# New ranks for the tasks of a kernel's opening, and products of a tile of ones on TensorE

## The chip, the cores and the metric

The kernel runs on one core of a Trainium2 chip. The time is that of the device, in microseconds (us), from the start of one execution to its end. Engines are named as the profile names them: PE is TensorE's matmul, PEld its load of the stationary operand, DVE is VectorE, ACT is ScalarE, POOL is GpSimd, and SP is SyncE, whose queue issues the DMAs. L12 is line 12 of the kernel; the changed kernel has a few lines more, so the same code stands some 3 to 15 lines further down there.

## The reference

Eight batches of an attention with two kinds of masks (a window of 32 keys in heads 0 to 3, every fourth of 128 keys in heads 4 to 7) feed a layer that turns the result by learned angles, mixes tokens and then channels:

```python
scores = scale * np.matmul(q, k.transpose(0, 1, 3, 2))
scores = np.where(masks[None, :, :, :], scores, -1000000000.0)
scores = scores - np.max(scores, axis=-1, keepdims=True)
attn = np.exp(scores)
attn = attn / (np.sum(attn, axis=-1, keepdims=True) + 1e-09)
x = np.matmul(attn, v)            # then (B, 8, 576, 64) -> (B, 576, 512)
theta = x @ w_theta
cos_t, sin_t = (np.cos(theta), np.sin(theta))
zr = x * cos_t
zi = x * sin_t
y = np.einsum('ts,bsd->btd', w_tok_r, zr) + np.einsum('ts,bsd->btd', w_tok_i, zi)
u = x + y
return u + np.maximum(u @ w_ch, 0.0)
```

Sequence 576, 512 channels. The four weights arrive as float64 and are turned into float32 on the chip.

## The kernel before, in words

**Work of a batch b.** The heads go in four pairs p. `scores(b, p)` multiplies a pair's queries and keys (PE, tile `s`, two halves of 5 and 4 blocks of 64 columns, the mask added either by products with `mskb` and `idb` on PE or on DVE), takes the row maxima (DVE, `mx`), the exponentials (ACT, `P`), the sums and their reciprocals (DVE, `sm`), and normalizes (POOL, L510). `turn(b, p)` transposes `P` into `pt` by DVE's 32x32 transposes, in batch 0 `flip` does it on PE; two `pt` tiles alternate between the pairs. `pv(b, p)` multiplies with the values (PE, tile `o`), ACT copies it out into `x`. `theta` multiplies `x` with the angle weights (tile `th`, five stripes of tokens in the order 4, 0, 1, 2, 3), `trig` takes sines and cosines on ACT (`g`, `K`) and multiplies by `x` on DVE, and `zsplit` splits each of the nine tiles `z` into a high part `zh` (ACT or DVE) and a low one `zl` (POOL). A unit `token(b, d, g)` is 27 products into a tile `y`, three for each `z` tile, in the order 0, 4, 1, 5, 2, 6, 3, 7, 8; there are eight units, four d in two halves g of the tokens. `residual` adds them to `x` (DVE, L825) and splits the sum into `u` (ACT, POOL). `chan(b, e, g)` is a unit of 12 products into a tile `c`. In names like `s1_3` or `y0_2` the first number is the batch, the second the pair or the d.

**Weights.** Each weight tile is loaded into a stage (`st_wth`, `st_wtk`, `st_wch`), clipped by DVE (L332), changed by ACT (L334 and L340, or DVE L337 for the second), put together by DVE (L342), and split by ACT (L350) and POOL (L352). The token weights are two sets of five tiles; those of the second half g = 1 (`st_wtk1`, split into `late_wt_a` and `late_wt_b`) and the channel weights (`st_wch`, `late_wc`) are staged in tiles that other weights or the first attention have used before: `st_wch0` needs the stage of `st_wtk1_2`, `st_wch1` that of `st_wtk1_3`, `st_wch2` that of `st_wch0`, `st_wch3` that of `st_wch1`. The DMA goes out only when POOL's split of the tile before has ended.

**Order.** What is done ahead of batch 1's own units is the opening: all of batch 0, the weights, the attention and the angles of batch 1, and two pairs of scores of batch 2. Its tasks are generators that name, step by step, an engine and a planned duration. While the program is written, `Order.run` plays them against each other: of the tasks ready for an engine it takes the one with the lowest rank, and pins the instruction at that place of the engine's order. `RANK` holds one number for each kind of task. So ranks change no instruction, only the order in which each engine and SP's queue run them; each engine works strictly in that order and waits where an operand isn't there. From the first product of `scores(2, 2)` on (PE, L468) the order comes from `phase`, written out by hand, and no rank has a say.

Of the kernel before, what the change touches and what calls it, by code (L numbers as in the profile page):

```python
# [8 lines left out]
F32 = mybir.dt.float32  # L9
F32R = mybir.dt.float32r  # L10
BF16 = mybir.dt.bfloat16
# [7 lines left out]
DM = H * D  # L19
# [10 lines left out]
EARLY = ("u0", "u1", "u2", "u3", "xh0")  # L30
LATE = ("u3", "xh1", "xh2", "xh3", "xh0")
LATE2 = ("xh2", "xh3", "xh2", "xh3")
RANK = dict(load=6.64, scores0=1.09, flip=0.01, pv0=1.13, pair=.21, theta_unpack=1.54, theta0=5.3, trig0=2.41,
            token_early=2.55, theta_split=6.42, token_late=6.75, chan=2.1, units=2.95, evacuate=4.49,
            scores1=4.02, scores2=7.3, pv1=8.0, theta1=5.96, trig1=7.42)
STS = (4, 0, 1, 2, 3)


FG0 = {4: ("zl2", "zl6"), 0: ("zl3", "zl7"), 1: ("zh3", "zh7")}
COS_PSUM, SIN_PSUM = True, True  # L40
KORD = (0, 4, 1, 5, 2, 6, 3, 7, 8)
TP0 = {4: "s", 0: "s", 1: "x", 2: "t", 3: "s"}
TP = {4: "t", 0: "s", 1: "s", 2: "t", 3: "s"}

# [17 lines left out]
class Order:  # L62
# [17 lines left out]
    def signal(self, event):  # L80
        self.events[event] = self.now

    def go(self, gen, rank=None):
        if not self.live:
            for _ in gen:
                pass
            return
        self.serial += 1
        t = [self.rank if rank is None else rank, self.serial, self.now, gen, None, 0.0]
        self.tasks.append(t)  # L90
        self.advance(t)
# [60 lines left out]
def build(ctx, tc, qT, kT, vw, wth, wtk, wch, maskb, ident, identb, outT):  # L152
    nc = tc.nc
    cp = ctx.enter_context(tc.tile_pool(name="const", bufs=1))
# [7 lines left out]
    ps_v = ctx.enter_context(tc.tile_pool(name="ps_v", bufs=1, space=PSUM))  # L162
# [7 lines left out]
    def pe(ins):  # L170
        tc.keep_in_program_order(ins)
# [13 lines left out]
    def reserve(tag):  # L185
        taken[tag] = taken.get(tag, -1) + 1
        return taken[tag]

    def take(tag, bufs, n=None):
        n = reserve(tag) if n is None else n  # L190
        if od.live:
            if n >= bufs:
                yield None, ("free", tag, n - bufs)
            if n:
                yield None, ("got", tag, n - 1)
            signal(("got", tag, n))
        return n

    def give(tag, n):
        if od.live:  # L200
            signal(("free", tag, n))

    def bank(tag, name):
        if tag == "v":
            n = yield from take(tag, 1)
            return ps_v.tile([128, 2 * DM], F32, tag=tag, name=name), (tag, n)
        pl, bufs = banks[tag]
        n = yield from take(tag, bufs)
        return pl.tile([128, DM], F32, tag=tag, name=name), (tag, n)
# [205 lines left out]
    def on_pe(b, pr):  # L415
        return b == 0 or (b, pr) in ((1, 2), (1, 3), (2, 0), (2, 1))
# [24 lines left out]
    def scores(b, pr):  # L441
# [161 lines left out]
    def pv(b, pr):  # L603
# [50 lines left out]
    def theta0(st):  # L654
        cs = slice(128 * st, min(128 * st + 128, S))
        n = cs.stop - cs.start
        for c in range(NC):
            yield None, ("wth32", c)
            yield None, ("xe", 0, c)
            if c == 0:  # L660
                if TP0[st] == "s":
                    yield None, ("sc", 0, NP - 1)
                elif TP0[st] in "tm":
                    yield None, ("fl", 0, NP - 1)
                ths[0, st] = yield from bank(TP0[st], f"th0_{st}")
# [170 lines left out]
    def token(b, d, g):  # L836
        yield None, ("z", b, KORD[0])
        yield None, ("wtk", g, KORD[0] // 2)
        ps, rel = yield from bank(unit_bank(b, NC * g + d), f"y{b}_{d}_{g}")
        ps = ps[:, :HS]  # L840
        cs = slice(128 * d, 128 * d + 128)
        n = 0
        for kt in KORD:
            yield None, ("z", b, kt)
            yield None, ("wtk", g, kt // 2)
            zh, zl = zs[b, kt]
            wh, wl = (w[:, HS * (kt % 2):HS * (kt % 2) + HS] for w in wtks[g, kt // 2])
            yield "PE", 369
            for l, r in ((zh, wh), (zh, wl), (zl, wh)):
                pe(nc.tensor.matmul(ps, l[:, cs], r, start=(n == 0), stop=(n == 3 * NK - 1)))  # L850
                n += 1
        signal(("tk", b, d, g))
        go(residual(b, d, g, ps, rel), RANK["evacuate"])

# [14 lines left out]
    def chan(b, e, g):  # L869
# [7 lines left out]
        for c in range(NC):  # L877
# [3 lines left out]
            for l, r in ((wchs[c][0], uh[b, c]), (wchs[c][0], ul[b, c]), (wchs[c][1], uh[b, c])):  # L881
                pe(nc.tensor.matmul(ps, l[:, cs], r[:, ts], start=(n == 0), stop=(n == 3 * NC - 1)))  # L882
                n += 1
        go(finish(b, e, g, ps, rel), RANK["evacuate"])

# [67 lines left out]
    EA, LA, LA2 = ([(t, reserve(t)) for t in ts] for ts in (EARLY, LATE, LATE2))  # L953
    XH = {p: reserve(f"xh{p}") for p in range(NP)}
    UH = {d: reserve(f"u{d}") for d in range(NC)}
    od.live = True
    go(first_loads(), 0)
    go(consts(), 0)
# [100 lines left out]
```

## Time and profile before

| what | value |
|---|---|
| time, median of 3 runs | 578.16 us (577.14 to 578.73) |
| time of the profiled execution | 577.82 us |
| its span, first to last instruction | 576.0 us |
| mean granted TensorE clock | 0.988 |
| busy shares PE, PEld, DVE, ACT, POOL | 96%, 87%, 66%, 60%, 39% |
| DMA | 81.91 MB, mean 142 GB/s |
| start of batch 2's third pair of scores on PE (end of the opening) | 143.01 us |

A row of the profile's timeline has start, duration, engine, line, operation, what it writes and reads, and how many equal ones it stands for; in brackets is the idle time of the engine just before it and what ended that. A row of windows has, for a stretch of time, its length, each engine's busy time and number of instructions, the clock that TensorE was granted (1.00 is full speed), the share of time the DMA engines moved data, and GB/s. A duration on PE overlaps with the next product's; how fast products follow each other is read from their starts.

### The profile page before, as it was taken

The numbers are of one execution on the slowest core, as the hardware profiler recorded it, in microseconds if no ns is written. First come the engines' busy times: TensorE is split into PE (matmuls) and PEld (weight loads), VectorE is DVE, ScalarE is ACT, GpSimd is POOL, SyncE is SP. The second block draws the span as 40 slices with busy tenths as digits, with TensorE's granted clock in tenths as the row PEclk, the third lists the DMA queues.
The fourth block names the chain that finished last, engine by engine and source line by source line (L and its number), as shares of the span: only waits on it lengthen the run. The fifth ranks groups of instructions, "written<-read, shape, count | busy, mean of one in ns | idle before, by whom it ended". The sixth has DMA issues, their size and how long they took to land.

```text
span 576.0 us, 13996 instructions
## 1 busy us (share of the span) xinstructions
PE 550.5 (96%) x5464; PEld 501.6 (87%) x5464; DVE 378.0 (66%) x1156; ACT 345.2 (60%) x939; POOL 222.2 (39%) x206
## 2 busy tenths in 40 slices
PE   5997799999999999999999999999999999999997
PEld 4744688879999899988999899988999899989997
DVE  3879798865666668756776768756775767445112
ACT  1498967768555784369555785359556695266110
POOL 2228855525224352226324253226323353325220
PEclk9999699899999999999999999999999999999999
DMA  8991437601747046540746146550747123321002
GB/s 303 400 368 28 165 105 245 216 0 63 231 150 193 32 162 210 169 127 20 268 143 172 64 148 202 181 136 11 252 146 190 69 83 102 77 89 65 18 1 83
DMA packets 45586, 81.91 MB, mean 142 GB/s; under 512 B 3920, under 2 KB 19024, under 8 KB 45520
## 3 DMA queue, kind: packets, MB, share of 16 engines
q1 hardware_dynamic: 45520, 81.02, 43.7%
q8 instruction: 43, 0.70, 0.5%
q14 instruction: 23, 0.19, 0.1%
HBM read 64.49 MB, written 16.52 MB: 141 GB/s over the span
## 4 chain that ended last, share of the span: by engine, by line
DVE 34%; ACT 30%; PE 25%; issue 5%; POOL 2%; DMA 2%; SPq 0%; ACTq 0%; POOLq 0%; DVEq 0%
DVE pt L525 16%; PE y L850 11%; ACT P L504 11%; PE c L882 6%; PE th L685 3%; DVE P L409 3%; ACT K L698 3%; ACT K L787 3%; DVE xh L599 3%; ACT th L796 2%; ACT zh L644 2%; DVE xq L729 2%; DVE K L789 2%; ACT cos L705 2%; ACT x L581 2%
## 5 line engine op out<-in xcount | busy, mean ns | idle before, releaser
L830 POOL TENSOR_TENSOR u<-x,u 128x288 fp32r<-128x288 f32 x64 | 54.7, 858 | 184.6 <-ACT u L828 184.6
L525 DVE STREAM_TRANSPOSE pt<-P 32x288 f32<-32x288 f32 x224 | 105.1, 469 | 12.0 <-POOL P L510 8.9
L882 PE MATMUL c<-u,late_wc 128*128 128x288 f32 x768 | 110.2, 296 | 2.8 <-DVE x L859 2.8
L882 PEld LDWEIGHTS c<-u,late_wc 128*128 128x128 f32 x768 | 106.0, 188 | 6.8 <-DVE x L859 4.0
L850 PE MATMUL y<-wtkh,zh 128*128 128x288 f32 x288 | 90.3, 314 | 1.1 <-ACT zh L644 1.1
L850 PE MATMUL y<-wtkh,zl 128*128 128x288 f32 x288 | 86.2, 299 | 4.0 <-POOL zl L646 4.0
L646 POOL TENSOR_TENSOR zl<-g,zh 128x512 fp32r<-128x512 f32 x40 | 52.3, 1316 | 97.5 <-ACT zh L644 84.5
L504 ACT ACTIVATE P<-P,mx 128x64 f32<-128x64 f32 x216 | 72.0, 335 | 25.8 <-DVE mx L498 25.8
L850 PE MATMUL y<-wtkl,zh 128*128 128x288 f32 x288 | 85.9, 298 | 0.0
L828 ACT CAST u<-x 128x288 fp32r<-128x288 f32 x64 | 26.9, 429 | 86.2 <-DVE x L825 85.5
L685 PE MATMUL th<-wthh,xh 128*128 128x512 f32 x224 | 74.8, 395 | 0.3 <-DVE g L784 0.3
L850 PE MATMUL y<-late_wt_b,zh 128*128 128x288 f32 x320 | 68.1, 297 | 0.0
L825 DVE TENSOR_TENSOR x<-y,x 128x288 f32<-128x288 f32 x64 | 28.1, 448 | 53.6 <-PE y L850 53.5
L850 PEld LDWEIGHTS y<-wtkh,zl 128*128 128x128 f32 x288 | 55.1, 191 | 4.7 <-POOL zl L646 4.7
L850 PEld LDWEIGHTS y<-wtkh,zh 128*128 128x128 f32 x288 | 54.9, 191 | 4.7 <-ACT zh L644 2.3
L850 PE MATMUL y<-late_wt_a,zh 128*128 128x288 f32 x256 | 56.3, 301 | 0.0
L850 PEld LDWEIGHTS y<-wtkl,zh 128*128 128x128 f32 x288 | 55.1, 191 | 0.3 <-issue 0.3
L510 POOL TENSOR_TENSOR P<-P,sm 128x576 f32<-128x576 f32 x32 | 37.5, 1172 | 41.1 <-DVE sm L508 18.1
L850 PEld LDWEIGHTS y<-late_wt_b,zh 128*128 128x128 f32 x320 | 51.4, 189 | 0.3
L685 PEld LDWEIGHTS th<-wthh,xh 128*128 128x128 f32 x224 | 42.0, 188 | 9.2 <-DVE g L784 0.6
L850 PE MATMUL y<-late_wt_b,zl 128*128 128x288 f32 x160 | 47.4, 296 | 0.0
L581 ACT COPY x<-o 128x576 f32<-128x576 f32 x32 | 29.4, 919 | 28.4 <-PE o L617 19.1
(108 smaller groups left out, 1106.3 us busy)
## 6 DMA issues: line engine op xcount, KB each, us to landing
q<-in_qT_dram SPq DMA_DIRECT2D x32, 576.0 KB, 5.2
va<-in_vw_dram SPq DMA_DIRECT2D x30, 320.0 KB, 3.2
k<-in_kT_dram SPq DMA_DIRECT2D x28, 304.0 KB, 5.5
out_dram<-x SPq DMA_DIRECT2D x28, 288.0 KB, 2.4
vb<-in_vw_dram SPq DMA_DIRECT2D x29, 256.0 KB, 3.8
xd<-xq SPq DMA_DIRECT2D x24, 288.0 KB, 5.1
xn<-xd SPq DMA_DIRECT2D x24, 256.0 KB, 3.4
st_wtk<-in_wtk_dram SPq DMA_DIRECT2D x8, 576.0 KB, 8.8
```

What stands on the lines that cost most here:

```text
L409: pin(nc.vector.tensor_tensor_reduce(out=P[:, n], in0=ps[:, n - g0], in1=mskb[:, mask_of(pr, n)], op0=ALU.add, op1=ALU.max, scale=1.0, sca ...
L504: table(nc.scalar.activation(P[:, n], P[:, n], AF.Exp, bias=mx[:, n:n + 1], scale=SCALE, accum_out=sm[:, n:n + 1]))
L510: pin(nc.gpsimd.tensor_tensor(P, P, sm.unsqueeze(2).to_broadcast([128, NJ, BW]), op=ALU.mult))
L525: pin(nc.vector.transpose(pmats[b, pr][k0:k0 + QB, :, hh, QB * e:QB * e + QB], P[p0:p0 + QB, :, QB * o:QB * o + QB]))
L581: pin(nc.scalar.copy(dst, src))
L646: pin(nc.gpsimd.tensor_tensor(lo, z, hi.bitcast(F32), op=ALU.subtract))
L685: pe(nc.tensor.matmul(pt, l, r, start=(n == 0), stop=(n == 3 * NC - 1)))
L825: pin(nc.vector.tensor_tensor(x[:, ts], ps, x[:, ts], op=ALU.add))
L828: pin(nc.scalar.copy(uh[b, d][:, ts], x[:, ts]))
L830: pin(nc.gpsimd.tensor_tensor(ul[b, d][:, ts], x[:, ts], uh[b, d][:, ts].bitcast(F32), op=ALU.subtract))
L850: pe(nc.tensor.matmul(ps, l[:, cs], r, start=(n == 0), stop=(n == 3 * NK - 1)))
L882: pe(nc.tensor.matmul(ps, l[:, cs], r[:, ts], start=(n == 0), stop=(n == 3 * NC - 1)))
```

## The change

The table `RANK` has new numbers. A tile `ones` (128x512, bf16) is set by DVE at the very start, and 14 products of it with itself go to PE ahead of everything else, into a tile `busy` that uses the PSUM banks of `o`. In the first token unit, `token(0, 0, 0)`, eight more such products stand ahead of the first product with `zh3`, and four ahead of the one with `zl3`. Nothing reads what they write.

```diff
-RANK = dict(load=6.64, scores0=1.09, flip=0.01, pv0=1.13, pair=.21, theta_unpack=1.54, theta0=5.3, trig0=2.41,
-            token_early=2.55, theta_split=6.42, token_late=6.75, chan=2.1, units=2.95, evacuate=4.49,
...
+RANK = dict(load=5.45, scores0=5.38, flip=0, pv0=0.8, pair=0.31, theta_unpack=2.69, theta0=2.39, trig0=2.41,
+            token_early=4.11, theta_split=8.74, token_late=5.88, chan=1.75, units=4.8, evacuate=2.41,
...
+WARM_UP = 14
...
+KEEP_BUSY = {(0, 0, 0, 3, 0): 8, (0, 0, 0, 3, 2): 4}
...
+            if (b, d, g, kt) == (0, 0, 0, KORD[6]):
+                busy = yield from bank("v", "busy")
             yield "PE", 369
-            for l, r in ((zh, wh), (zh, wl), (zl, wh)):
+            for i, (l, r) in enumerate(((zh, wh), (zh, wl), (zl, wh))):
+                for _ in range(KEEP_BUSY.get((b, d, g, kt, i), 0)):
+                    pe(nc.tensor.matmul(busy[0][:, :DM], ones[:, :128], ones, start=True, stop=True))
                 pe(nc.tensor.matmul(ps, l[:, cs], r, start=(n == 0), stop=(n == 3 * NK - 1)))
                 n += 1
+        if b == d == g == 0:
+            give(*busy[1])
...
+    ones = cp.tile([128, DM], BF16, name="ones")
+    nc.vector.memset(ones, 1.0)
+    busy = ps_v.tile([128, 2 * DM], F32, tag="v", name="busy")
+    for n in range(WARM_UP):
+        pe(nc.tensor.matmul(busy[:, :DM], ones[:, :128], ones, start=True, stop=True))
```

The orders show what the ranks move. From `scores(2, 2)` on, PE has the same order before and after. Three places ahead of it follow.

**ACT, from the angles of stripe 2 to the last high part `zh0_3`.** Before:

```order
L350 CAST wthh1_653<-st_wth1_97 128x512
L644 CAST zh0_1_665<-K0_1_597 128x512
L796 ACTIVATE g0_2_642<-K0_2_641 128x512
L350 CAST wthh2_672<-st_wth2_98 128x512
L698 ACTIVATE K0_2_641<-K0_2_641 128x512
L787 ACTIVATE K0_3_686<-th0_3_534 128x512
L705 ACTIVATE K0_2_641<-K0_2_641,halfpi_95 128x512
L350 CAST wthh3_684<-st_wth3_99 128x512
L796 ACTIVATE g0_3_687<-K0_3_686 128x512
L644 CAST zh0_2_713<-K0_2_641 128x512
```

After, up to `zh0_3`:

```order
L708 ACTIVATE K0_2_639<-K0_2_639,halfpi_95 128x512
L701 ACTIVATE K0_3_664<-K0_3_664 128x512
L337 ACTIVATE st_wtk1_0_629<-st_wtk1_0_629 128x576
L708 ACTIVATE K0_3_664<-K0_3_664,halfpi_95 128x512
L647 CAST zh0_2_759<-K0_2_639 128x512
L507 ACT_TABLE_LOAD
L507 ACTIVATE P1_0_559,sm1_0_561<-P1_0_559,mx1_0_560 128x64 x3
L343 ACTIVATE st_wtk1_0_629<-st_wtk1_0_629 128x576
L647 CAST zh0_3_797<-K0_3_664 128x512
```

The splits of three angle weights (`wthh1` to `wthh3`) have moved from among the sines to behind the second half's token weights, some twenty rows further on; `zh0_2` has moved behind the last sine (L705, now L708), and two more steps on `st_wtk1` stand ahead of that sine than before (`st_wtk1_1`'s second and `st_wtk1_0`'s first).

**PE, in the units `y0_2` and `y0_3` of the first half.** The first product with batch 1's values, `o1_0`, stood here before:

```order
L850 MATMUL y0_3_0_956<-wtkh0_515,zl0_0_613 128x288
L617 MATMUL o1_0_904<-pt0_107,va1_0_434 64x64 x10
L617 MATMUL o1_0_904<-pt0_107,vb1_0_435 64x64 x8
L850 MATMUL y0_3_0_956<-wtkh2_569,zh0_4_576 128x288
L850 MATMUL y0_3_0_956<-wtkl2_570,zh0_4_576 128x288
```

After, it stands after nine products of the unit before, ahead of the scores `s1_2`:

```order
L857 MATMUL y0_2_0_913<-wtkh0_532,zl0_1_687 128x288
L620 MATMUL o1_0_919<-pt0_124,va1_0_451 64x64 x10
L620 MATMUL o1_0_919<-pt0_124,vb1_0_452 64x64 x8
L857 MATMUL y0_2_0_913<-wtkh2_571,zh0_5_668 128x288
L857 MATMUL y0_2_0_913<-wtkl2_572,zh0_5_668 128x288
L857 MATMUL y0_2_0_913<-wtkh2_571,zl0_5_669 128x288
L427 LDWEIGHTS idb_94
L427 MATMUL s1_2_0_923<-mskb_93,idb_94 128x64
```

`o1_0` has moved up by 21 products of token units, and `o1_1` in the same way from the 24th to the sixth product of `y0_3`. The scores `s1_2` stand six products earlier, the first half of `s1_3` where it stood, its second half 18 products later, behind the ninth product of the second half's first unit.

**DVE, from the maxima of batch 1's third pair to the first channel weight.** Before:

```order
L525 STREAM_TRANSPOSE pt1_109<-P1_1_724 32x9x32 x2
L430 TENSOR_REDUCE mx1_2_906<-s1_2_0_908 128x5
L525 STREAM_TRANSPOSE pt1_109<-P1_1_724 32x9x32 x2
L438 TENSOR_SCALAR mx1_2_906<-mx1_2_906 128x5
L430 TENSOR_REDUCE mx1_2_906<-s1_2_5_940 128x4
L825 TENSOR_TENSOR x0_2_407<-y0_2_0_883,x0_2_407 128x288
L438 TENSOR_SCALAR mx1_2_906<-mx1_2_906 128x4
L342 SCALAR_TENSOR_TENSOR st_wtk1_2_409<-st_wtk1_2_409 128x576
L342 SCALAR_TENSOR_TENSOR st_wtk1_3_479<-st_wtk1_3_479 128x576
L342 SCALAR_TENSOR_TENSOR st_wtk1_4_698<-st_wtk1_4_698 128x288
```

After:

```order
L345 SCALAR_TENSOR_TENSOR st_wtk1_3_496<-st_wtk1_3_496 128x576
L528 STREAM_TRANSPOSE pt1_126<-P1_1_719 32x9x32 x2
L345 SCALAR_TENSOR_TENSOR st_wtk1_4_672<-st_wtk1_4_672 128x288
L528 STREAM_TRANSPOSE pt1_126<-P1_1_719 32x9x32 x2
L433 TENSOR_REDUCE mx1_2_921<-s1_2_0_923 128x5
L528 STREAM_TRANSPOSE pt1_126<-P1_1_719 32x9x32 x2
L441 TENSOR_SCALAR mx1_2_921<-mx1_2_921 128x5
L433 TENSOR_REDUCE mx1_2_921<-s1_2_5_993 128x4
L335 TENSOR_SCALAR st_wch0_963<-st_wch0_963 128x512
L828 TENSOR_TENSOR x0_2_424<-y0_2_0_913,x0_2_424 128x288
L441 TENSOR_SCALAR mx1_2_921<-mx1_2_921 128x4
```

The joins of `st_wtk1_2` to `st_wtk1_4` (L342, now L345) have moved from behind both maxima to ahead of the first (that of `st_wtk1_2` stands further up, ahead of the last two transposes of `pt0`). The clip of the first channel weight, `st_wch0` (L332, now L335), stood 15 rows behind the second maximum; now it is the next row, and two rows behind it stands the L441 for the second half of `s1_2`, without which ACT can't take those exponentials. The other three channel weights have moved up likewise, and in SP's queue `st_wch0` from behind the second load of batch 2's queries to ahead of the first.

More of the change, by code (lines that the diff above doesn't have):

```diff
@@ L32 @@
 LATE2 = ("xh2", "xh3", "xh2", "xh3")
-RANK = dict(load=6.64, scores0=1.09, flip=0.01, pv0=1.13, pair=.21, theta_unpack=1.54, theta0=5.3, trig0=2.41,
-            token_early=2.55, theta_split=6.42, token_late=6.75, chan=2.1, units=2.95, evacuate=4.49,
-            scores1=4.02, scores2=7.3, pv1=8.0, theta1=5.96, trig1=7.42)
+RANK = dict(load=5.45, scores0=5.38, flip=0, pv0=0.8, pair=0.31, theta_unpack=2.69, theta0=2.39, trig0=2.41,
+            token_early=4.11, theta_split=8.74, token_late=5.88, chan=1.75, units=4.8, evacuate=2.41,
+            scores1=5.5, scores2=2.39, pv1=0.3, theta1=4.18, trig1=3.32)
 STS = (4, 0, 1, 2, 3)
```

## The prediction

> **What bounds the kernel now.** I read the page first, then windows, then PE's waits.
>
> ```profile
> span 576.0 us, 13996 instructions
> PE   5997799999999999999999999999999999999997
> DVE  3879798865666668756776768756775767445112
> PEclk9999699899999999999999999999999999999999
> ```
>
> ```profile
> 62.00:90.00 28.00, 24.74 (x276) 22.31 (x275) 23.80 (x62) 23.19 (x94) 19.35 (x16) 0.90 0.38 127
> 90.00:125.00 35.00, 31.81 (x311) 28.27 (x309) 29.43 (x68) 24.00 (x66) 15.38 (x14) 0.95 0.47 160
> 125.00:150.00 25.00, 24.89 (x240) 22.91 (x242) 13.09 (x41) 20.04 (x46) 12.39 (x11) 1.00 0.26 86
> 150.00:300.00 150.00, 148.91 (x1575) 140.22 (x1570) 107.57 (x383) 89.59 (x265) 52.80 (x50) 1.00 0.50 152
> ```
>
> From slice 10 on PE is full: 148.91 of 150 us, at full clock. That part keeps its order, so nothing can be won there; what counts is when it begins:
>
> ```profile
> 143.01 1.27 PE L468 MATMUL s<-k,q 128*64 128x64 f32 x36
> ```
>
> Ahead of it PE has gaps, and from 62 to 125 us DVE is busy 53.2 of 63 us (23.80 + 29.43), nearly as long as PE. PE's waits from 50 to 143 us, with the number and the longest, and the clock around them:
>
> ```profile
> PE y L850 <- POOL zl L646: 4.0, 3, 1.5
> PE s L424 <- ACT P L485: 3.0, 2, 2.0
> PE y L850 <- ACT zh L644: 1.1, 1, 1.1
> PE xn L759 <- DVE K L750: 1.0, 1, 1.0
> PE th L685 <- DVE g L784: 0.3, 1, 0.3
> ```
>
> ```profile
> 66.70:67.80 1.10, 1.01 (x7) 1.00 0.00 0
> 67.80:71.30 3.50, 3.50 (x17) 0.51 0.00 0
> 71.30:75.30 4.00, 4.00 (x32) 1.00 0.00 0
> 101.50:105.20 3.70, 3.69 (x32) 0.56 0.85 267
> ```
>
> Once the last low part, `zl0_3`, is there (PE goes on at 66.79), PE still loses 3.0 + 1.0 + 0.3 = 4.3 us by waits, 3.5 x 0.49 = 1.7 by half clock behind the waits for the last sines, and 3.7 x 0.44 = 1.6 by half clock behind the wait for scores at 101.51: 7.6 us in all. That is the most that a better order behind `zl0_3` could win.
>
> **The change, step by step.** I follow one quantity: how much later the changed kernel reaches a place with the same work of PE done. Each product of a token unit counts 0.133 us (32 in 4.00 us above), `o` 1.2, a half of scores with masks 0.9 or 0.75.
>
> *The first 14 products.* They run while PE would wait for the first keys.
>
> ```profile
> 7.03 1.34 PE L468 MATMUL s<-first_k,q 128*64 128x64 f32 x20 [3.62 <-DMA first_k<-in_kT_dram]
> 13.63 1.34 PE L468 MATMUL s<-first_k,q 128*64 128x64 f32 x20
> 18.02 0.80 PE L468 MATMUL s<-first_k,q 128*64 128x64 f32 x20
> 10.27 1.35 PE s L468 x20
> ```
>
> No row shows a product of ones. At half clock 288 columns take 3.5/17 = 0.21 to 0.24 us, so 512 take some 0.4 and 14 end by about 7.1 us, at full clock they end at half of that; neither delays the keys of 7.03 by more than the two mask products (0.45). Scores at full clock save 0.54 us for 20. But the second pair's start at 10.27 is set by a DMA (the chain of waits has `first_k` up to there), and the gaps between the loads then open wider, in which the clock may fall again. Bounds: +0.3 (the masks come late) to -1.2 (two of four pairs gain); I take **-0.3**, near the row at 10.27, which the clock can't move.
>
> *ACT up to the last high part.*
>
> ```profile
> 54.85 0.66 ACT L350 CAST wthh<-st_wth 128x512 fp32r<-128x512 f32 x1
> 58.39 0.63 ACT L796 ACTIVATE g<-K 128x512 f32<-128x512 f32 x1 [0.68 <-DVE K L789]
> 60.04 0.72 ACT L334 ACTIVATE st_wtk<-st_wtk 128x576 f32<-128x576 f32 x1
> 60.66 0.71 ACT L705 ACTIVATE K<-K,halfpi 128x512 f32<-128x512 f32 x1
> 62.03 1.28 ACT L504 ACT_TABLE_LOAD   x1
> 64.47 0.62 ACT L644 CAST zh<-K 128x512 fp32r<-128x512 f32 x1
> 65.17 1.57 POOL L646 TENSOR_TENSOR zl<-K,zh 128x512 fp32r<-128x512 f32 x1 [0.61 <-ACT zh L644]
> 66.79 0.40 PE L850 MATMUL y<-wtkh,zl 128*128 128x288 f32 x1 [1.11 <-POOL zl L646]
> ```
>
> Ahead of the last sine (60.66) four casts go (three `wthh`, `zh0_2`), 0.53 to 0.57 each by starts, 2.2 us; two steps of `st_wtk1` come, 0.62 each (60.04 to 60.66): -1.0. Between that sine and `zh0_3` stood 3.8 us; now the sine 0.62, `zh0_2` 0.53, a table load 1.28, three exponentials 1.15 (63.32 to 64.47), L343 0.62: 4.2, so +0.4. The wait of 0.68 at 58.39 is for a DVE step that now has fewer rows ahead of it: -0.5. POOL's `zl0_3` started right behind `zh0_3`, so taking a split off POOL gives nothing more. Sum **-1.1**; with the first term `zl0_3` comes 1.4 earlier.
>
> *Products of ones among the last sines.* Eight and four at 0.2 to 0.4 us stand in two waits of 1.1 us. If they overrun, `y0_0` ends up to 1.5 us later, and if they hold the clock, the 1.7 us at half clock go. I cost both at **nothing**: the cover is the chain on DVE, which starts its transposes 3.1 us behind `zl0_3` (66.79 to 69.88), once ACT, DVE and POOL have finished `P1_0`, and PE gets to wait for them, next paragraph. Without that cover it would be -1.7 to +1.5.
>
> *`o1_0`, and DVE up to the third pair's maxima.*
>
> ```profile
> 68.69 1.15 POOL L510 TENSOR_TENSOR P<-P,sm 128x576 f32<-128x576 f32 x1 [0.61 <-DVE sm L508]
> 69.88 0.95 DVE L525 STREAM_TRANSPOSE pt<-P 32x288 f32<-32x288 f32 x2 [1.02 <-POOL P L510]
> 72.40 1.25 DVE L342 SCALAR_TENSOR_TENSOR st_wtk<-st_wtk 128x576 uint32<-128x576 uint32 x1
> 79.02 0.49 DVE L430 TENSOR_REDUCE mx<-s 128x5 f32<-128x320 f32 x1
> 81.39 1.79 DVE L342 SCALAR_TENSOR_TENSOR st_wtk<-st_wtk 128x576 uint32<-128x576 uint32 x3
> 82.47 0.31 PE L424 MATMUL s<-mskb,idb 128*128 128x64 bf16 x5 [1.04 <-ACT P L485]
> ```
>
> PE gets to `o1_0` 7 + 27 + 9 products behind `zl0_3`, 5.7 us; its `pt0` needs DVE's 3.1, eight transposes at 0.48, `sm` 0.5 and one join of 0.6 to 1.25: 8.3. So PE now waits 2.6 us there, where it waited for nothing before. This costs the end nothing yet, because the maxima `mx1_2` are later still: three joins (1.79 together, longer where POOL works beside them, as at 72.40) have come ahead of them, one transpose pair and one join of 72.40's kind have left: **+1.1**. So the maximum comes at 79.02 - 1.4 + 1.1 = 78.7 and the masks of `s1_3` at 82.2, with `o1_1` (1.2 us) already done: 1.5 us ahead.
>
> *Channel weights among the scores.*
>
> ```profile
> 95.71 0.80 PE L617 MATMUL o<-pt,va 128*64 128x64 f32 x20
> 105.36 0.43 DVE L332 TENSOR_SCALAR st_wch<-st_wch 128x512 f32<-128x512 f32 x1 [1.03 <-DMA st_wch<-in_wch_dram]
> 107.86 0.80 PE L617 MATMUL o<-pt,va 128*64 128x64 f32 x20
> DMA to landing us min/median/max: 3.6/4.7/5.6
> ```
>
> Behind the exponentials of `s1_2`'s first half (end at 82.0) ACT now has two `xh`, one `x`, one split and three steps on `st_wch` (some 0.6 each, like the rows of 54.85 and 60.04) and `u` (0.3), 4.6 us, before those of the second half (1.15): 87.8. PE gets to the second half of `s1_3`, whose bank they free, at 82.2 + 4.5 = 86.7 and waits 1.1: **1.1 us ahead** (I count `s1_3`'s missing half against it). Then POOL normalizes `P1_2` up to 89.4 (1.15 as at 68.69, and 0.45 for `sm`), and DVE's eight transposes (3.85), one maximum (0.4), the clip of `st_wch2` (0.4), one residual and a small row (0.6) take 5.3, with 0.5 for the load: 95.2, where PE waits for `o1_2` since 93.4. The old kernel was there at 95.71, but with `s2_0` done and six products fewer: **0.4 behind**. Next, `o1_3`: from 95.2 DVE has two joins (1.3) and a clip (0.4) of channel weights, `sm` (0.4), what is left of POOL's `P1_3` (0.8), two maxima (0.9), the split of `xh1_2` (0.9), a residual (0.5), eight transposes (3.8) and some 0.5 of handing over, 9.5 us: 104.7; PE waits 1.5. The old kernel was there at 107.86, because it lost 2.0 by the wait at 101.51 and 1.6 by the clock behind it, and had then 9 products fewer but `s2_1` done: **2.8 ahead**.
>
> *To the end of the opening.* Batch 1's angles now come earlier among the channel units, so the waits of 1.0 and 0.3 should go: **3.7 ahead** with what little else differs left out. Of the four new waits (2.6, 1.1, 1.9, 1.5) only the last has PE alone behind it; if the clock falls there as at 101.5, that costs 1.6. I add half: **-2.9**.
>
> The Trainium skill says otherwise of this last term. In "TensorE: Matmul & The Clock Gate", Part 1, the clock goes back to half only after a whole idle window of about 3.4 us; no wait here is that long, so by that rule the sum would be -3.7. In this trace it fell behind waits of 1.1 twice and of 1.95 once, so the measurement decides.
>
> **The sum** stands against the profiled execution, 577.82 us (1.82 around its span): 574.9. The median of the runs shown is 0.34 above it: **575.3**.
>
> **The rivals.** *The new waits are shorter than I made them*: ACT takes casts in gaps, and only the wait at `o1_0` stays. Then -1.4 - 7.6 + 2.6 = -6.4: 571.8. For it speaks that each of my waits adds up rows without seeing where they overlap; against it, DVE's 84% from 62 to 125 us. *All is taken back*: the first products gain nothing (+0.3), DVE's wait at 58.39 stays (+0.5), the last clock fall costs fully (+0.8), the wait for `xn` stays (+1.0): 577.9. For it speaks that each of these is in the old trace. That the change doesn't do what it says, a clock that stays half in spite of the ones, is in it, since I gave little for the clock. *Slower*: DVE, in order, stops at each clip of a channel weight until its load lands. `st_wch0` can be issued only when POOL has split `st_wtk1_2`, at some 77.6 us, and lands 3.6 to 5.6 later, while DVE is there at about 81; I counted 0.5 for each of four. If SP's queue, in which these loads stand behind loads of keys and values, issues them 1.5 us later than POOL allows, DVE loses 4 x 1.5 = 6.0: 581.3. It decides from about 1.2 us on, where 4.6 us are lost and the whole is above 579.9.
>
> **How the numbers follow.** A measurement of this kernel can tell about 0.3% (1.7 us) from no change: faster is below 576.4, slower above 579.9. The forecast has 0.50, its own range 573.4 to 577.2, with 0.08 of that above 576.4. Shorter waits have 0.20, all taken back 0.20, slower 0.10. So faster 0.42 + 0.20 = 0.62, within 0.3% 0.28, slower 0.10. The range takes in the first three cases with their unknowns (1.5 us either way on the outer ones): 570.3 to 579.6.
>
> **What would show it.** PE's timeline: `s2_2`'s start at about 140 us instead of 143.01; scores of 20 products at 0.80 instead of 1.34 from 7 us on, if the ones hold the clock; 1.00 in the window behind `zl0_3`; a wait of some 2.6 us ahead of the first `o` behind it, ended by DVE `pt`; 1 to 2 us ahead of the next scores and values; DVE waiting for `st_wch` by DMA for less than 1 us each. I am wrong if PE has no wait at `o1_0`, if those DMA waits pass 1.2 us each, or if PE's share from 150 us on differs.

## The result, and the profile after

| | before | after |
|---|---|---|
| median of 6 runs each | 577.56 us (576.37 to 578.73) | 581.79 us (580.65 to 582.36) |
| profiled execution, its span | 577.82 us, 576.0 us | 581.52 us, 579.7 us |

The ratio is 1.0071, with a 95% interval of 1.0055 to 1.0088: the changed kernel is slower by 4.2 us, where 2.9 us less was predicted.

From the page of the changed kernel:

```profile
span 579.7 us, 14051 instructions
PE   7897978999999999999999999999999999999997
PEclk9999879999999999999999999999999999999999
```

Its windows, with the columns as before:

```profile
62.00:90.00 28.00, 23.67 (x241) 19.97 (x242) 22.91 (x53) 22.46 (x73) 18.69 (x16) 0.88 0.36 125
90.00:125.00 35.00, 32.13 (x338) 28.93 (x337) 28.96 (x67) 25.57 (x88) 16.77 (x16) 1.00 0.49 157
125.00:150.00 25.00, 23.90 (x180) 21.70 (x179) 15.07 (x43) 17.03 (x32) 11.50 (x9) 1.00 0.18 59
150.00:300.00 150.00, 148.88 (x1595) 140.21 (x1594) 105.17 (x365) 92.60 (x279) 53.78 (x51) 1.00 0.51 156
```

From 150 us on nothing has changed (PE 148.88 of 150 us, before 148.91). The difference lies ahead of it, in the opening, whose end is the start of batch 2's third pair of scores in PE's timeline:

```profile
146.35 1.27 PE L471 MATMUL s<-k,q 128*64 128x64 f32 x36
```

That is 3.34 us later than the 143.01 of before; the span has grown by 3.7. From 62 to 90 us PE gets 241 products done, 35 fewer than before and eleven of them products of ones (a few records of a trace can be missing), at a clock of 0.88; from 90 to 125 it has full clock and makes up a part. PE's waits from 50 to 147 us:

```profile
PE o L620 <- DVE pt L528: 6.1, 3, 3.3
PE s L471 <- DVE K L792: 2.0, 1, 2.0
PE y L857 <- POOL zl L649: 1.3, 2, 1.0
PE xn L762 <- DVE g L753: 1.0, 1, 1.0
PE o L620 <- issue: 0.7, 1, 0.7
```

The waits for `zl`, `zh` and `P` (8.1 us) have shrunk to 1.3. Instead there are now waits of 6.1 for the transposes, ahead of the products with the values, 0.7 at the same place whose end the profile doesn't explain ("issue" stands for that), and 2.0 for the angles' `K`.

### The profile page after: what moved, and what is told of

It reads as the page before. It is cut to its first block, busy times and chain, and to the rows that moved or that the text cites. A ratio compares the mean times of both kernels' runs of the same rounds, so it can differ in the third digit from the quotient of the medians.

```text
span 579.7 us, 14051 instructions
## 1 busy us (share of the span) xinstructions
PE 554.4 (96%) x5489; PEld 502.3 (87%) x5490; DVE 380.1 (66%) x1157; ACT 345.7 (60%) x939; POOL 221.4 (38%) x206
## 4 chain that ended last, share of the span: by engine, by line
DVE 34%; ACT 28%; PE 28%; issue 5%; POOL 2%; DMA 2%; SPq 0%; POOLq 0%; ACTq 0%; DVEq 0%
DVE pt L528 16%; PE y L857 11%; ACT P L507 10%; PE c L891 6%; DVE P L412 3%; PE th L688 3%; DVE xh L602 3%; ACT K L701 3%; ACT K L790 2%; ACT th L799 2%; PE th L670 2%; POOL P L513 2%; ACT zh L647 2%; DVE K L792 2%; DVE xq L732 2%
## 6 DMA issues: line engine op xcount, KB each, us to landing
q<-in_qT_dram SPq DMA_DIRECT2D x32, 576.0 KB, 5.0
st_wtk<-in_wtk_dram SPq DMA_DIRECT2D x8, 576.0 KB, 8.5
```

## The experiments

Two causes offered themselves: the new wait at `o1_0` with the half clock behind it (PE; A in the expectations), and the joins that now stand ahead of the third pair's maxima (DVE; B). Later a third came in, ACT's order between the two halves of `s1_2`'s exponentials (E). All ratios are to the kernel before, with 95% intervals; the edits are to the changed kernel unless another is named.

### What of PE, DVE and the products costs it

**e1_hold**: PE is kept busy with 18 products of ones in the wait ahead of `o1_0`, nothing else moves.

```diff
+        if (b, pr) == (1, 0):
+            for _ in range(18):
+                pe(nc.tensor.matmul(ps[:, :DM], ones[:, :128], ones, start=True, stop=True))
         for j in range(NJ):
```

> The changed kernel with 18 more products of ones on PE directly ahead of o1_0, nothing else moved. They fill the wait at o1_0 (73.2 to 76.8 us), so the clock should stay at 1.00 behind it, where it was 0.5 for 5.5 us. Theory A (the loss is PE's wait at o1_0 of 4.0 us and the half clock behind it, 2.8 us): about 2.5 us faster than the changed kernel, 579. Theory B (the loss is DVE's chain, which reaches the first maximum of s1_2 only at 82.2 us, whatever PE does before): 0 to 0.5 us faster, 581.3 to 581.8.

Measured: 581.22 us, 1.0062 (1.0044 to 1.0080). The clock held: from 75.75 to 82.50 us the windows of the changed kernel and of this one read

```profile
75.75:82.50 6.75, 5.69 (x66) 5.04 (x66) 6.21 (x13) 4.40 (x8) 6.75 (x6) 0.50 0.46 159
```

```profile
75.75:82.50 6.75, 6.63 (x102) 5.40 (x101) 6.51 (x12) 4.26 (x8) 6.75 (x6) 1.00 0.51 147
```

so PE had 3.4 us more of full clock, and then stood still. Its timeline, at the masks of `s1_3` and at `o1_2`:

```profile
86.36 0.31 PE L427 MATMUL s<-mskb,idb 128*128 128x64 bf16 x5 [0.71 <-ACT P L488]
...
100.28 1.22 PE L623 MATMUL o<-pt,va 128*64 128x64 f32 x17 [2.31 <-DVE pt L528]
```

The masks come 1.4 us earlier than the 87.79 of the changed kernel, and now with a wait for ACT; `o1_2` comes 0.9 earlier. What PE loses at `o1_0` is at most a small part of what the end waits for: the time is near theory B's, and A's 579 is outside the interval.

**e2_no_joins**: the three joins of `st_wtk1_2` to `st_wtk1_4` are left out.

```diff
-        pin(nc.vector.scalar_tensor_tensor(out=Ti, in0=Ci, scalar=3, in1=Ti,
+        if not (name == "wtk1_" and n >= 2):
+            pin(nc.vector.scalar_tensor_tensor(out=Ti, in0=Ci, scalar=3, in1=Ti,
```

> The changed kernel without the three DVE joins of st_wtk1_2, st_wtk1_3 and st_wtk1_4 (L345; 1.62, 0.86 and 1.21 us in its trace); these weights are therefore not the reference's. All other instructions stand in the same order. Theory A: only the join inside the transposes of pt0 counts, the wait at o1_0 gets 1.6 us shorter and the time falls by 1.6 us, to about 580. Theory B: the first maximum of s1_2 comes 3.7 us earlier, if PE's scores are there, which now come 1.6 us earlier, so 3 us or less are won: 578.5 to 579.5, and the masks of the first half of s1_3 stand near 85 instead of 87.79 us.

Measured: 579.55 us, 1.0040 (1.0026 to 1.0055), about half of the loss given back. In DVE's timeline the first maximum of `s1_2`, and in PE's the two halves of `s1_3`:

```profile
79.02 0.49 DVE L434 TENSOR_REDUCE mx<-s 128x5 f32<-128x320 f32 x1
```

```profile
84.95 0.32 PE L428 MATMUL s<-mskb,idb 128*128 128x64 bf16 x5
...
91.87 0.28 PE L428 MATMUL s<-mskb,idb 128*128 128x64 bf16 x4 [2.01 <-ACT P L489]
```

The maximum is back at the 79.02 of the old kernel, 3.5 us ahead of the changed one, and the first half of `s1_3` 2.8 ahead. But the second half still waits for ACT and comes at 91.87 (92.60 in the changed kernel): a second chain holds there.

**e3_late_o**: `pv1=8.0`, the old rank, in place of the new one, so that the products with batch 1's values stand further back on PE.

> The changed kernel with the rank pv1 as before the change (8.0 instead of 0.3): o1_0 goes behind the scores s1_2 on PE, o1_1 likewise later; DVE keeps its order up to the second maximum of s1_2. Theory A: the wait at o1_0 and the half clock behind it go, 3 to 4 us won, 577.5 to 578.5. Theory B: DVE is at the first maximum at 82.2 us as in the changed kernel, PE only waits later, at the first half of s1_3, for its exponentials until about 86.2 us: 0.3 to 1.6 us won there, 580 to 581.5.

Measured: 582.63 us, 1.0088 (1.0072 to 1.0105). The wait at `o1_0` fell to 0.24 us, and a longer one came at the next place:

```profile
86.62 0.42 PE L427 MATMUL s<-mskb,idb 128*128 128x64 bf16 x5 [5.03 <-ACT P L488]
```

In the changed kernel, in e1 and here, with PE early or late, at full clock or half, these masks come at 87.8, 86.4 and 86.6. So up to here DVE and ACT set most of the time and PE at most the 1.4 us between them, as in e1. The whole came out slower than either theory allowed; what its order costs behind this place was not looked into.

**e4_ranks_only**: the new ranks with no product (the tile and its memset stay).

```diff
-WARM_UP = 14
+WARM_UP = 0
-KEEP_BUSY = {(0, 0, 0, 3, 0): 8, (0, 0, 0, 3, 2): 4}
+KEEP_BUSY = {}
```

> The changed kernel without any product of ones (neither the first 14 nor the twelve among the last sines); the order of everything else is the same. Theories A and B: the half clock behind the last sines comes back (1.7 us), but PE then only waits less at o1_0, and the first scores fall back to 1.34 us for 20, which a DMA hides: 0 to 0.5 us slower than the changed kernel, 581.8 to 582.3. Theory C (the products themselves cost the time): faster by 2 us or more, below 579.8.

Measured: 581.12 us, 1.0056 (1.0043 to 1.0070). Without the products 3.5 of the 4.2 us of loss are still there, so at most a small part of it is theirs.

**e5_ones_only**: the old table `RANK` with all 26 products.

> The kernel before, with its own ranks, plus the products of ones (14 at the start, eight and four among the last sines); the order of everything else is that of before. Theory P (the products win what they fill): the half clock behind the last sines goes (1.7 us) and the time falls to 576. Theory D (DVE's chain to the maxima of s1_2 hides PE's clock there): within 0.5 us of before, 577.1 to 578.1. Theory C (the products cost time): above 578.5.

Measured: 579.66 us, 1.0030 (1.0014 to 1.0046). They didn't help the old order either: slower by 1.6 us, though its profiled execution had full clock throughout the opening.

### ACT's order, and the channel weights

Why the second half of `s1_3` is late shows in ACT's timeline of the changed kernel, where the exponentials of `s1_2`'s two halves begin:

```profile
84.70 0.32 ACT L488 ACTIVATE P<-s,mx 128x64 f32<-128x64 f32 x1 [3.00 <-DVE mx L441]
...
91.29 0.29 ACT L488 ACTIVATE P<-s,mx 128x64 f32<-128x64 f32 x1
```

Its maxima are there at 85.93 (L441, 85.77 + 0.16). Between the halves stand `xh` twice, three steps on `st_wch`, one `x`, one `u`, the split of the first channel weight and a wait for DVE.

**e6_exp_first**: these exponentials become a task of their own with a rank of 0.1, ahead of all weights.

```diff
+    def exponentials(b, pr, held, P, mx, sm):
...
-            for g0, (ps, rel) in held.items():
...
+            go(exponentials(b, pr, held, P, mx, sm), 0.1)
+            yield None, ("ex", b, pr)
```

> The changed kernel with the exponentials of batch 1's and 2's masked pairs as tasks of their own with a rank ahead of all others: on ACT those of s1_2's second half stand behind one cast instead of nine instructions, on DVE the maximum of s1_3's first half comes ahead of the splits of xh1_1. Theory E (what ACT and DVE have between the two halves of s1_2's exponentials, 86.4 to 91.3 us, sets P1_2, pt0 and o1_2): these exponentials come some 4 us earlier, PE no longer waits 2.36 us at o1_2, and 2 to 2.5 us are won, 579.3 to 579.8. Theory F (DVE's sum of work is the bound, in whatever order): less than 0.7 us won, above 581.

**e7_chan7**: `chan=7.0`, the channel weights behind everything else of the opening.

> The changed kernel with the rank chan at 7.0 instead of 1.75: the steps of the channel weights on ACT and DVE go behind the exponentials, maxima and transposes of batch 1's pairs. Theory E: the exponentials of s1_2's second half come 2 to 3 us earlier (three steps of st_wch0 and one of st_wch1 are gone from ahead of them, the casts of xh stay), 1.5 to 2.5 us won, 579.3 to 580.3, if the channel weights are not late at the first channel unit; if they are, PE waits there on late_wc and nothing is won. Theory F: less than 0.7 us won.

**e8_both**: as e6, and the joins of `st_wtk1_2` to `st_wtk1_4` may come only behind the third pair's maxima.

```diff
+        if name == "wtk1_" and n >= 2:
+            yield None, ("mask", 1, 2, 5)
         yield "DVE", dve(sz)
```

> The changed kernel with the exponentials ahead as in e6 and with the joins of st_wtk1_2 to st_wtk1_4 held back until the maxima of s1_2 have been taken (their work is all there). Theory E with the joins' share as e2 measured it (2.2 us): both parts add, 4 to 4.5 us won, 577.3 to 577.8, as fast as before the change or a little faster. Theory F: the joins come back later and cost the same, above 580.

Measured: e6 582.66 us, 1.0077 (1.0058 to 1.0095); e7 586.07 us, 1.0140 (1.0121 to 1.0160); e8 583.03 us, 1.0083 (1.0063 to 1.0103). None gave anything back. PE's timeline of e6, at `o1_2`, the first `xn`, and `s2_2`:

```profile
97.91 0.74 PE L625 MATMUL o<-pt,va 128*64 128x64 f32 x17 [0.38 <-DVE pt L533]
...
126.94 1.02 PE L767 MATMUL xn<-idt,x 128*128 128x128 f32 x4 [1.91 <-DVE g L758]
...
147.87 1.27 PE L481 MATMUL s<-k,q 128*64 128x64 f32 x36
```

and of e8, at `o1_2` and two channel units:

```profile
93.99 0.74 PE L627 MATMUL o<-pt,va 128*64 128x64 f32 x17 [1.14 <-DVE pt L535]
...
117.07 0.66 PE L898 MATMUL c<-u,late_wc 128*128 128x288 f32 x3 [0.73 <-DVE x L835]
...
124.07 0.67 PE L898 MATMUL c<-u,late_wc 128*128 128x288 f32 x3 [1.31 <-DVE x L875]
```

Both chains can be broken: `o1_2` moves from 101.15 to 97.91 and 93.99 (with 1.6 and 3.2 us less of PE's work ahead of it, counted in products as in the prediction). Of e8's 7.2 us another 1.2 belong to its start: the product with `zl0_3` stands at 65.35 instead of 66.58, though nothing is moved ahead of it; some 2.7 remain. The time doesn't follow. What has been put back on ACT and DVE is missed later: in e6 in a longer wait for the angles and half clock behind it, in e8 in waits for the residuals of channel units, and in e7 in waits of 2.7 and 1.7 us for the channel weights themselves. In e7 `o1_3` comes at 106.86, 4.0 us earlier, with 3.3 us less of PE's work ahead of it; so the early channel weights hold up the pairs by little, and behind everything else they cost more. A place in between, such as the old rank of 2.1 by itself, was not tried.

All three came out as theory F's numbers said, but its reason doesn't fit: DVE's sum of work hasn't grown. From 62 to 125 us it is busy 51.9 us (22.91 + 28.96), where it was 53.2 before the change. The order makes the loss, and no single chain of it was found that holds the end.

### Which ranks, which products

**e9_early_new** and **e10_late_new** have no products (the tile stays). The first has the new numbers from `load` to `token_early` and the old ones from `theta_split` to `trig1`, the second the reverse.

> No products of ones; the nine ranks from load to token_early are the changed ones, the ten from theta_split to trig1 those of before. DVE and ACT then keep before's order behind the last sines: one join ahead of the maxima of s1_2, and two instructions between its exponentials. Theory G (the loss comes from the late ranks, which put joins, channel weights and splits of xh between the steps of batch 1's third and fourth pair): within 1 us of before, a ratio of 0.998 to 1.002. Theory H (the early ranks lose as well): 1.5 us or more slower.

> No products of ones; the nine ranks from load to token_early are those of before, the ten from theta_split to trig1 the changed ones. DVE has three joins ahead of the maxima of s1_2 and the clip of st_wch0 and the split of xh1_0 among them, ACT nine instructions between the exponentials of its two halves. Theory G: slower by what the ranks cost without products (e4: ratio 1.0056), 1.004 to 1.007. Theory H: 1 to 2 us less than that, 1.002 to 1.004.

Measured: 579.67 us, 1.0045 (1.0029 to 1.0062), and 583.57 us, 1.0094 (1.0070 to 1.0118). Either half of the new numbers makes the old table slower, as theory H said, and the late half by more than either theory gave and no less than both together (e4 and e14). So the loss is not the sum of what the two halves cost by themselves, and neither half alone is to blame. Apart from `pv1` and `chan` (e3 and e7) no single rank was tried.

**e11_warm_only** and **e12_busy_only** are the old table with the first 14 products alone (`KEEP_BUSY = {}`), and with the later 8 + 4 alone (`WARM_UP = 0`).

> The kernel before with the 14 products at the start alone; the order of everything else is that of before. Theory D (the loads hide what the faster first scores win): within 0.5 us of before. Theory P (the clock at the start wins): 0.5 to 1.2 us faster. Theory K (these products are what made e5 slower): 1 to 1.7 us slower.

> The kernel before with the eight and four products among the last sines alone; the order of everything else is that of before. Theory D (DVE's chain to the maxima of s1_2 hides PE's clock): within 0.5 us of before. Theory P (the clock behind the last sines wins 1.7 us of PE): 1 to 1.7 us faster. Theory K (these are what made e5 slower, by keeping the last products with zh3 and zl3 back): 1 to 1.7 us slower.

Measured: 580.06 us, 1.0041 (1.0027 to 1.0054), and 580.22 us, 1.0040 (1.0021 to 1.0059). Each alone costs no less than both together, more than theory K gave. Since e5, e11 and e12 share the tile `ones`, which moves nearly all other tiles in SBUF, the next four separate the tile from the products and from the ranks.

**e13_tile_only** is the old table with tile and memset but no product; **e14_pure_ranks** is the kernel before with the new table alone; **e15_ones_end** (old table, all products) and **e16_after_end** (the changed kernel) have the tile behind all others, so that nothing is moved:

```diff
+    op = ctx.enter_context(tc.tile_pool(name="ones", bufs=1))
...
-    ones = cp.tile([128, DM], BF16, name="ones")
+    ones = op.tile([128, DM], BF16, name="ones")
```

> The kernel before with the tile ones and its memset at the start, and no product; every engine's order is that of before apart from this one memset, but the tile lies ahead of nearly all others in SBUF and moves 590 of 599 places by 1024 bytes. Theory M (the place of the tiles costs the time): 2 to 2.9 us slower than before, a ratio of 1.0035 to 1.005. Theory L (the memset ahead of DVE's first work costs it): the same. Theory N (the products and the early ranks each cost it, the tile nothing): 0.999 to 1.001.

> The kernel before with the changed ranks alone: no tile ones, no memset, no product. Every engine's order is that of e4 (ranks without products) apart from the memset; no place is moved by 1024 bytes. Theories M and L: 2 us or more faster than e4, a ratio to before of 1.001 to 1.003. Theory N: as e4, 1.005 to 1.006.

> The kernel before with all 26 products as in e5, but the tile ones lies behind all other tiles in SBUF, so that none is moved. Theory M: 1 to 2.5 us faster than e5, 0.999 to 1.001 of before, or a little under it if the clock that the products hold wins something. Theories L and N: as e5, 1.002 to 1.005.

> The changed kernel with the tile ones behind all other tiles in SBUF; every engine's order is that of the changed kernel. Theory M: 2 to 2.5 us faster than the changed kernel, 1.002 to 1.004 of before. Theories L and N: as the changed kernel, 1.006 to 1.008.

| | old ranks | new ranks |
|---|---|---|
| no tile, no product | 1 | e14 1.0065 (1.0044 to 1.0085) |
| tile, no product | e13 1.0008 (0.9995 to 1.0020) | e4 1.0056 (1.0043 to 1.0070) |
| tile and products | e5 1.0030 (1.0014 to 1.0046) | after 1.0071 (1.0055 to 1.0088) |
| products, nothing moved | e15 1.0036 (1.0022 to 1.0049) | e16 1.0068 (1.0046 to 1.0091) |

The tile's place and its memset cost nothing that can be told from noise (L and M fall, N holds). The ranks alone cost 0.56 to 0.65%, 3.5 and 4.3 us in e4 and e14, nearly the whole. The products cost the old order 0.3 to 0.4% in four kernels (e5, e11, e12, e15), and the new order 0.03% (e16 against e14) to 0.15% (after against e4), which the intervals don't tell from nothing.

**What stays open** is how the products cost the old order its 1.6 to 2.9 us. They keep the clock at the places where they stand, as meant. Of one execution each, e12 has its last sine at 61.72 us and e13 at 59.91, though up to there both run the same order; their clocks rose at different times (below). With one profile of each kernel, what the products did and what that execution did can't be told apart.

One part can be seen. In e5, PE stops in the middle of the first `o`, behind the 22nd of 36 products:

```profile
19.14 0.62 PE L620 MATMUL o<-pt,first_v 128*64 128x64 f32 x14 [1.39 <-issue]
```

and again for 1.16 us at 25.55, behind the 22nd product of a flip; nothing that the profile shows ended these waits. The changed kernel, e1, e2, e7 and e16 stop at the same two products, for 1.0 to 1.6 and 0.9 us. All these have the first 14 products, and full clock at these places. In the kernels without them, e13 among them with full clock from 13.46 us on, PE has no such wait there. But e8 has them too, with full clock, and only 0.2 us at the second place. What it is stays open.

## Why the prediction was wrong

The places that the prediction named, in the order in which the changed kernel passes them:

| place | predicted | measured | late by | of that, new |
|---|---|---|---|---|
| product with `zl0_3` | 65.4 (66.79 - 1.4) | 66.58 | 1.2 | 1.2 |
| first maximum of `s1_2` | 78.7 | 82.50 | 3.8 | 2.6 |
| masks of `s1_3` | 82.2 | 87.79 | 5.6 | 1.8 |
| its second half | 87.8 | 92.60 | 4.8 | -0.8 |
| `o1_2` behind its wait | 95.2 | 101.15 | 6.0 | 1.2 |
| `o1_3` behind its wait | 104.7 | 110.86 | 6.2 | 0.2 |
| `s2_2` | 140.1 (143.01 - 2.9) | 146.35 | 6.2 | 0.0 |

From the masks of `s1_3` on the sums hold within 1.2 us each. The miss is made ahead of them, and the step that failed first and most is **"*`o1_0`, and DVE up to the third pair's maxima*: +1.1"**.

*DVE up to the maximum: +1.1, measured +3.7* (82.50 against 79.02, with `zl0_3` only 0.2 earlier). DVE's timeline of the changed kernel, from the first transpose to the step without which ACT has no exponentials to do:

```profile
70.49 0.95 DVE L528 STREAM_TRANSPOSE pt<-P 32x288 f32<-32x288 f32 x2 [1.02 <-POOL P L513]
...
74.14 1.62 DVE L345 SCALAR_TENSOR_TENSOR st_wtk<-st_wtk 128x576 uint32<-128x576 uint32 x1
...
78.13 0.86 DVE L345 SCALAR_TENSOR_TENSOR st_wtk<-st_wtk 128x576 uint32<-128x576 uint32 x1
...
80.01 1.21 DVE L345 SCALAR_TENSOR_TENSOR st_wtk<-st_wtk 128x288 uint32<-128x288 uint32 x1
...
82.50 0.49 DVE L433 TENSOR_REDUCE mx<-s 128x5 f32<-128x320 f32 x1 [0.30 <-PE s L471]
...
84.01 0.57 DVE L441 TENSOR_SCALAR mx<-mx 128x5 f32<-128x5 f32 x1
```

and POOL's splits beside the joins:

```profile
73.69 1.45 POOL L355 TENSOR_TENSOR late_wt_a<-st_wtk,late_wt_a 128x576 fp32r<-128x576 f32 x1
...
76.93 1.44 POOL L355 TENSOR_TENSOR late_wt_b<-st_wtk,late_wt_b 128x576 fp32r<-128x576 f32 x1
...
79.61 1.29 POOL L355 TENSOR_TENSOR wthl<-st_wth,wthh 128x512 fp32r<-128x512 f32 x1
```

By its parts, the +1.1 held the three joins at 3.3 us (1.1 + 0.95 + 1.25), less a pair of transposes and a join that were to leave. Five errors add up to the 2.6 that were missing. The pair of transposes, 0.95, has not left: 14 transposes stand ahead of the maximum in both orders, before in runs of 2, 2, 8 and 2, of which the third is

```profile
73.67 3.85 DVE L525 STREAM_TRANSPOSE pt<-P 32x288 f32<-32x288 f32 x8
```

The first of them starts 3.9 us behind `zl0_3`, not 3.1: 0.8. That is a wait of ACT, in the middle of the exponentials, for DVE's `mx` (L501, which took 1.23 us there and 0.28 before, and ended with POOL's `zl0_3`):

```profile
66.59 0.35 ACT L507 ACTIVATE P<-P,mx 128x64 f32<-128x64 f32 x1 [0.82 <-DVE mx L501]
```

The joins took 1.62 + 0.86 + 1.21 = 3.69: 0.4, since each ends only after POOL's running operation has (POOL's three end at 75.14, 78.37 and 80.90, the joins at 75.76, 78.99 and 81.22: 0.62 behind the first two, and 0.32 for the third, half as wide). DVE's wait for the scores, whose products ran at half clock (20 in 1.34), is 0.3, and the small rows of `sm` took 0.15 longer. e2 measured the joins by themselves: the maximum comes 3.5 us earlier, and 4.1 counted from `zl0_3`, which stands at 67.20 there. So their gross price was nearly right, and one of them did leave; but the pair of transposes credited against it did not.

Of the joins' wait for POOL the Trainium skill says in "SBUF — State Buffer", section "Who interferes with whom": an instruction of DVE with two inputs in SBUF and one of GpSimd that reads SBUF lock each other out of a shared pair of ports. A join has two inputs, and the trace agrees with the rule by the 0.62 and 0.32 above; the transposes, with one input, took 0.95 a pair beside POOL's splits or not.

For the forecast the right prices would have been enough, since the sums behind the masks hold. That this step makes the loss is shown in part. Leaving the joins out (e2) gives back 2.2 us, about half of it. Moving them behind the maximum (e8) gives nothing back; what was put back is missed later. What the other half hangs on, and what holds the end in e6 to e8, stays open.

*Behind the maximum to the masks of `s1_3`: 1.8 more.* 0.4 of it is L441, which took 0.57, before 0.17: it ended at 84.58, right behind a split of POOL that ended at 84.56. It has one input, so the rule on two inputs doesn't explain it. The rest is PE, which waited 0.7 ("issue") + 3.3 = 4.0 us at `o1_0` where I had 2.6 (the transposes start 0.8 later, and the join among them took 1.62 where I had 0.6 to 1.25), and was at half clock for 6.75 us behind that:

```profile
76.81 1.22 PE L620 MATMUL o<-pt,va 128*64 128x64 f32 x17 [3.28 <-DVE pt L528]
...
87.79 0.32 PE L427 MATMUL s<-mskb,idb 128*128 128x64 bf16 x5
...
101.15 0.74 PE L620 MATMUL o<-pt,va 128*64 128x64 f32 x17 [2.36 <-DVE pt L528]
...
110.86 0.74 PE L620 MATMUL o<-pt,va 128*64 128x64 f32 x17 [0.51 <-DVE pt L528]
```

I covered that wait by DVE's chain, and e1 and e3 bear the cover out up to 1.4 us: without the half clock or without the wait, the masks come at 86.4 and 86.6 instead of 87.8, held by ACT.

*ACT up to the last high part: -1.1, measured -0.3* for `zh0_3`, and -0.2 for `zl0_3`:

```profile
59.35 0.74 ACT L337 ACTIVATE st_wtk<-st_wtk 128x576 f32<-128x576 f32 x1 [1.22 <-DVE st_wtk L335]
59.98 0.71 ACT L708 ACTIVATE K<-K,halfpi 128x512 f32<-128x512 f32 x1
...
64.15 0.61 ACT L647 CAST zh<-K 128x512 fp32r<-128x512 f32 x1
```

The last sine came 0.7 earlier (60.66 before), where -1.5 was predicted. A wait of 1.22 for the clip of a token weight, one of the two steps that I counted at 0.62, stands right ahead of it: the time of the casts that left went mostly into this wait. Behind the sine my +0.4 came true (59.98 to 64.15 is 4.2).

*The first 14 products: -0.3, measured some -0.1.* The scores run at 0.80 for 20 at once, but the first `o` stops in its middle:

```profile
6.53 0.80 PE L471 MATMUL s<-first_k,q 128*64 128x64 f32 x20 [0.44 <-DMA first_k<-in_kT_dram]
...
9.89 0.80 PE L471 MATMUL s<-first_k,q 128*64 128x64 f32 x20 [1.14 <-DMA first_k<-in_kT_dram]
...
18.38 0.62 PE L620 MATMUL o<-pt,first_v 128*64 128x64 f32 x14 [1.06 <-issue]
```

The second pair is 0.4 earlier (10.27 before, a row that I had taken for one that the clock can't move) and waits longer for its load, as argued. The fourth pair's scores, at 15.83, are 2.2 earlier than the 18.02 of before; then come the waits of 1.06 at 18.38 and of 0.89 at 24.51 that the profile doesn't explain, which no kernel without the products has. The first stripe's angles, at 36.16, are 0.1 earlier (36.30 before).

*Products among the last sines: nothing*, not contradicted in the new order (e4 against after, both groups of products together). They held the clock, 0.99 from 62.00 to 75.75, and the half clock only came later, behind the new wait at `o1_0`. That products cost the old order 0.3 to 0.4% I had not thought possible beyond the bound of 1.5 us of an overrun.

*Channel weights: the sizes held.* From the end of the first half's exponentials to the second half's I counted 4.6 us, and 86.2 to 91.29 is 5.1; from `o1_2` to `o1_3` I counted 9.5, and 9.7 it was; the longest wait of DVE for a load of `st_wch` there was 0.34 us. The **slower rival** (581.3) came close by its number and not by its mechanism: the stalls of 1.5 us for each load aren't there. **Shorter waits** (571.8) and **all taken back** (577.9) lie 10.0 and 3.9 us below what was measured.

*To the end of the opening: luck.* The 0.0 of the table's last row is two errors that cancel: the wait of 1.0 for `g`, which was to go, stayed (0.97, at 126.59), and the half clock behind `o1_3`, which I had at 0.8, didn't come (1.00 from 90 to 150 us).

Four figures of the prediction are wrong without changing its outcome. The wait of 1.0 for `K` that it counts behind `zl0_3` stands at 59.10, ahead of it; one as long, for `g`, stands at 125.11. 32 products in 4.00 us are 0.125 each, and 0.133 is the distance of their starts. 2.8 and the waits of 1.0 and 0.3 make 4.1, not 3.7. And 577.9 + 1.5 is 579.4, not 579.6.

The range fell short too: its top is 2.2 us under the 581.8, only one rival ended clearly above the time before, and none asked what it costs if the chain that I let cover PE's new wait is itself late.

## What to carry to other kernels

When an order is changed on an engine that others wait for, count its instructions up to the next hand-over one by one in both orders, those credited as leaving above all, and price each by a row in which its new neighbours run beside it. A change that trades waits on one chain for work on another is worth what the latest chain says; here breaking both late chains (e8) brought `o1_2` forward by some 2.7 us at equal work of PE and the time by nothing, because what had been put back was missed later. And products that keep the clock up are to be measured by themselves: here they held it and gained nothing that was measured.

## What the runs showed of the hardware

*When the clock falls.* Almost equal waits are followed by a fall or by none. In PE's timeline of e13 and of e15, which run the same order there:

```profile
100.79 0.30 PE L427 MATMUL s<-mskb,idb 128*128 128x64 bf16 x2 [2.00 <-ACT P L488]
...
101.41 0.80 PE L471 MATMUL s<-k,q 128*64 128x64 f32 x20
```

```profile
102.55 0.30 PE L428 MATMUL s<-mskb,idb 128*128 128x64 bf16 x2 [2.41 <-ACT P L489]
...
103.17 0.94 PE L472 MATMUL s<-k,q 128*64 128x64 f32 x20
```

Behind 2.00 us the scores go on at 0.80 for 20, behind 2.41 the clock falls (0.94 for 20, and half speed in what follows), and in the kernel before it fell behind 1.95. The prediction's "waits of 1.1 twice" stand ahead of one fall, at 67.8; another, at 57.6, came behind a wait of 1.52 (56.52). Once down, it stayed down for some 3.4 us or twice that: 6.75 us from 75.75 to 82.50 in the changed kernel, 3.50 from 67.80 in the kernel before. "TensorE: Matmul & The Clock Gate", Part 1, of the Trainium skill has a free-running window of 3.4 us; the lengths agree with that, and the falls behind waits of 1.1 to 2.4 us don't agree with its whole idle window.

*How much one execution's clock can shift the rest.* The kernel before, e13 and e12 run the same order up to the last sine. The first half of the third pair's scores in PE's timelines, and for e12 of the fourth's (before's rows, 13.63 with 1.34 and 18.02 with 0.80, are in the prediction):

```profile
13.46 0.80 PE L471 MATMUL s<-first_k,q 128*64 128x64 f32 x20
```

```profile
13.74 1.34 PE L471 MATMUL s<-first_k,q 128*64 128x64 f32 x20
...
19.08 1.06 PE L471 MATMUL s<-first_k,q 128*64 128x64 f32 x20
```

e13 is at full speed by 13.46 us, the kernel before by 18.02, e12 only behind 19.08; the last sines follow at 59.91, 60.66 and 61.72, and `s2_2` at 142.25, 143.01 and 145.61. That the one makes the other is likely by its order and not shown: e5, at full clock all along, has its last sine at 61.61, with the waits of 1.39 and 1.16 us told above on its way.
